# How many weight slices the first pass of layer one takes in the first three blocks of tokens: 3, 4 and 6 in place of 5, 5 and 7

## The chip, the cores and the metric

The kernel runs on one core of a Trainium2 chip. The metric is the time of one execution on the device in microseconds (us). The core's engines are called as the profile calls them: PE (matrix products; PEld are its weight loads), DVE (vector), ACT (activations), POOL (GpSimd) and SP, whose queue issues every DMA of this kernel.

## The reference

Attention over 8 batches of 576 tokens, 8 heads of 64, whose keys and values are first averaged in groups of 8 (so 72 keys per head), and two feed-forward layers behind it, all in fp32:

```python
scores = scale * q @ mean8(k).T ; attn = softmax(scores) ; x = attn @ mean8(v)
x = x.transpose(0, 2, 1, 3).reshape(4608, 512)      # tokens x (heads * 64)
h = x @ w_in1 ; x = (h * cos(h)) @ w_out1           # 512 -> 2048 -> 512
h = x @ w_in2 ; out = (h * clip(h + 3, 0, 6) / 6) @ w_out2
```

The weights arrive as 64-bit floating-point numbers, read as pairs of 32-bit words.

## The kernel before, in words

The 4608 tokens are cut into 9 blocks of 512, which don't coincide with the batches of 576. A block of a layer needs all 16 slices of 128 of the 2048 hidden features. One slice of one block is a *step*: a first GEMM (`gemm1`, line 175) of 12 matmuls, the activation, and two steps later a second GEMM (`gemm2`, line 237) of 12 matmuls, which adds into the block's four accumulators. It is 12 since every operand is split into a high and a low part (4 chunks, 3 products each). A step is also two half-steps, called slots: the even one has the first GEMM of step s, the odd one the second GEMM of step s - 2.

The activation of a step of layer one is three operations of ACT (lines 185, 195, 199), two of DVE (196, 209), the high part on ACT (212) and the low part (218) on POOL, or on DVE for the step numbers listed in `GLD`. ACT uses Sin there and Exp in the attention, and loads a table whenever it changes between them.

Layer one goes over the blocks twice. Pass one (the list `NAL`) takes the first slices of each block, `NAL[block]` of them, and stores the partial sums to memory. Pass two takes the rest, adds the partial sums and stores the layer's result. The reason is room: while the attention is live, there is space for the converted weights of 7 slices only. Layer two then takes all 16 slices of each block.

A weight slice has two halves. A half is fetched (512 KB, `fetch_weights`, two in flight) and converted (`convert_weights`) from the 64-bit words to a high and a low part: four operations of DVE (lines 116, 120, 125, 128), two of ACT (115, 133) and one of POOL (134). When that happens follows three things: a count of attention pieces for the first six halves (`WPRE`), due slots for the next five (`WAT`, line 53: 5, 10, 13, 13, 19), and need: a step whose slice isn't whole yet converts it at once, and each step also asks for the next step's slice (`need`, lines 613 to 619, called on lines 667 and 674). After the attention the rest is converted one operation to a slot (`w_ahead`).

The attention is a generator of 253 pieces (a piece ends at each `yield` of lines 514 to 547): scores, exponentials, normalisation, transposes, and the product with v, whose result is stored to memory as x (line 503) and fetched again by blocks (line 145), split in a high and a low part by ACT (152) and POOL (153). The keys and values pass through one buffer each in turn (line 334 averages them on DVE). 39 pieces come before step 0. From then on each slot lets the generator run up to a goal, which depends on the block and on how far the block has come:

```python
goal = base + 32 * (key[1] + (2 * i + odd + 1 + PACE) / (2 * NAL[key[1]]))   # line 708
goal += GOFF[slot]                                                           # line 712
```

`key[1]` is the block, `i` the step within it, `base` is 39. So 32 pieces go to each block, whatever its number of steps. The x of the next block is fetched when at most four steps of the block are left and the batch that it needs is done (lines 688 to 691).

The order of writing is a wish. A planner puts the instructions on each engine in an order of its own ahead of time, by that order and by what it expects to be ready, so that matmuls of a later step stand between those of the attention.

Of the kernel before, what the change touches and what calls it, by code (L numbers as in the profile page):

```python
# [29 lines left out]
def tile_kernel(ctx, tc, q, k, v, wi1, wo1, wi2, wo2, ident_d, mask_d, out):  # L30
# [8 lines left out]
    NF = wo1.shape[0] // P  # L39
    NB = NT // N  # L40
    NA = 7
    NAL = [5, 5, 7, 7, 7, 7, 7, 7, 7]
    LAG = 2
    GLD = [18, 23, 24, 28, 30, 37, 38, 39, 40, 41, 42, 43, 44, 45, 46, 47, 48, 49, 50, 51, 52, 53, 54, 55, 56, 57, 58, 60, 61, 62, 63, *range(64, 999)]
    LEAD = 1
# [514 lines left out]
    for bl in range(NB):  # L560
        n = NAL[bl]
        steps += [(0, (0, bl), bl, fc, fc == 0, fc == n - 1) for fc in range(n)]
    SA = len(steps)
    for bl in range(NB):
        n = NAL[bl]
        steps += [(0, (1, bl), bl, fc, fc == n, fc == NF - 1) for fc in range(n, NF)]
# [94 lines left out]
    for slot in range(2 * (T + LAG) + 4):  # L661
# [43 lines left out]
        if live:  # L705
            key = steps[s][1]
            i = sum(1 for x in steps[:s] if x[1] == key)
            goal = base + 32 * (key[1] + (2 * i + odd + 1 + PACE) / (2 * NAL[key[1]]))
            if key[0] > 0:
# [65 lines left out]
```

## Time and profile before

| | before |
|---|---|
| median of 3 runs | 1803.48 us (1799.16 to 1804.42) |
| profiled execution | 1801.62 us |
| its span, first to last instruction | 1799.8 us |
| DVE, ACT, POOL busy | 896.4, 891.6, 393.8 us |

The page cuts the span into 40 slices of 45 us; a digit is the busy share of a slice in tenths:

```profile
PE   5689999999999999999999999999999999999999
DVE  6998656656777656654446852222222222222222
ACT  3588878787666655555556543232323222232222
POOL 2755444222223222221112421010101000010000
```

The attention is live in the first ten slices, layer one's second pass and layer two take the rest. Matmuls overlap in the profile, so a PE digit of 9 may hide a matmul that is short of its pace; a busy share is compared with that of other stretches, not with one.

### The profile page before, as it was taken

The page shows a single profiled execution, that of the slowest core. Times are in us where ns is not written, and L with a number is a line of the kernel's source. Part 1 is how long each engine was busy: PE and PEld are TensorE (multiplying, and loading weights), DVE is VectorE, ACT ScalarE, POOL GpSimd, SP SyncE. Part 2 cuts the span into 40 slices and gives each one's busy share as a digit, 9 for nine tenths or more (in the row PEclk, how much of TensorE's full clock was granted, in tenths as well). Part 3 has the DMA queues.
Part 4 walks back from the last instruction along what each step waited for, and adds up shares of the span by engine and source line. Part 5 has one row for each costly group of instructions (what it writes and reads, how often), then busy time and mean ns, then how long its engine had stood idle before and what let it go on. Part 6 is the DMA issues. An engine that isn't in the chain of part 4 may idle for free.

```text
span 1799.8 us, 21002 instructions
## 1 busy us (share of the span) xinstructions
PE 1739.2 (97%) x7952; PEld 1429.5 (79%) x7952; DVE 896.4 (50%) x1398; ACT 891.6 (50%) x1508; POOL 393.8 (22%) x320
## 2 busy tenths in 40 slices
PE   5689999999999999999999999999999999999999
PEld 4567777788888888888888788888888888888887
DVE  6998656656777656654446852222222222222222
ACT  3588878787666655555556543232323222232222
POOL 2755444222223222221112421010101000010000
PEclk7799999999999999999999999999999999999999
DMA  7656442323333313222223411010101010100000
GB/s 196 194 172 195 143 136 74 118 83 103 117 105 118 106 59 105 97 85 76 71 70 106 140 59 47 1 47 1 47 1 48 0 47 8 40 18 24 0 24 24
DMA packets 115077, 139.84 MB, mean 78 GB/s; under 512 B 44192, under 2 KB 68896, under 8 KB 114976
## 3 DMA queue, kind: packets, MB, share of 16 engines
q1 hardware_dynamic: 114976, 138.51, 24.8%
q8 instruction: 62, 1.02, 0.2%
q14 instruction: 39, 0.32, 0.1%
HBM read 100.73 MB, written 37.75 MB: 77 GB/s over the span
## 4 chain that ended last, share of the span: by engine, by line
PE 85%; DVE 6%; DMA 3%; POOL 2%; ACT 2%; issue 2%; SPq 0%; DVEq 0%; POOLq 0%; ACTq 0%
PE y L237 40%; PE h L175 40%; PE ap_ps L494 1%; PE ap_ps L407 1%; DVE raw L334 1%; DMA raw<-in_k_dram 1%; DMA raw<-in_v_dram 1%; POOL xl L153 1%; DVE sm L429 1%; DVE g L196 1%; POOL e L433 1%; DVE a L125 1%; PE ap_ps L393 0%; PE ap_ps L459 0%; DVE sm L430 0%
## 5 line engine op out<-in xcount | busy, mean ns | idle before, releaser
L175 PE MATMUL h<-xl,wh 128*128 128x512 f32 x1152 | 451.3, 392 | 4.2 <-POOL xl L153 4.2
L175 PE MATMUL h<-xh,wh 128*128 128x512 f32 x1152 | 453.5, 394 | 0.5 <-DVE g L209 0.5
L175 PE MATMUL h<-xh,wl 128*128 128x512 f32 x1152 | 450.8, 391 | 0.0
L201 DVE SCALAR_TENSOR_TENSOR g<-g,h 128x512 f32<-128x512 f32 x144 | 99.3, 689 | 454.7 <-ACT g L187 454.7
L153 POOL TENSOR_TENSOR xl<-xr,xh 128x512 fp32r<-128x512 f32 x108 | 153.3, 1438 | 779.2 <-ACT xh L152 778.1
L187 ACT ACTIVATE g<-h,bias_c 128x512 f32<-128x512 f32 x144 | 99.0, 687 | 409.7 <-PE h L175 409.3
L218 DVE TENSOR_TENSOR gl<-g,gh 128x512 fp32r<-128x512 f32 x255 | 190.3, 746 | 157.7 <-ACT gh L212 154.4
L212 ACT ACTIVATE gh<-g 128x512 fp32r<-128x512 f32 x288 | 181.6, 630 | 175.2 <-DVE g L201 104.5
L175 PEld LDWEIGHTS h<-xl,wh 128*128 128x128 f32 x1152 | 216.7, 188 | 50.2 <-POOL xl L153 6.5
L175 PEld LDWEIGHTS h<-xh,wh 128*128 128x128 f32 x1152 | 216.9, 188 | 45.5 <-issue 1.2
L175 PEld LDWEIGHTS h<-xh,wl 128*128 128x128 f32 x1152 | 216.9, 188 | 44.3
L237 PE MATMUL y<-gh,wh 128*128 128x512 f32 x576 | 226.7, 394 | 0.0
L237 PE MATMUL y<-gl,wh 128*128 128x512 f32 x576 | 226.6, 393 | 0.0
L237 PE MATMUL y<-gh,wl 128*128 128x512 f32 x576 | 225.6, 392 | 0.0
L237 PE MATMUL y<-wh,gh 128*128 128x512 f32 x576 | 224.3, 389 | 1.1 <-DVE yv L245 1.1
L237 PE MATMUL y<-wh,gl 128*128 128x512 f32 x576 | 224.1, 389 | 0.0
L237 PE MATMUL y<-wl,gh 128*128 128x512 f32 x576 | 224.1, 389 | 0.0
L196 DVE SCALAR_TENSOR_TENSOR g<-g,t 128x512 f32<-128x512 f32 x144 | 112.6, 783 | 149.8 <-ACT g L195 149.5
L134 POOL TENSOR_TENSOR wl<-a,wh 128x512 fp32r<-128x512 f32 x64 | 88.4, 1381 | 269.4 <-ACT wh L133 269.4
L237 PEld LDWEIGHTS y<-wh,gh 128*128 128x128 f32 x576 | 108.2, 188 | 24.4 <-DVE yv L245 1.9
L199 ACT ACTIVATE g<-g 128x512 f32<-128x512 f32 x144 | 91.0, 632 | 72.9 <-DVE g L196 72.5
L237 PEld LDWEIGHTS y<-wh,gl 128*128 128x128 f32 x576 | 108.1, 188 | 22.5
(110 smaller groups left out, 2086.1 us busy)
## 6 DMA issues: line engine op xcount, KB each, us to landing
xr<-x_d SPq DMA_DIRECT2D x72, 256.0 KB, 3.2
st<-in_moe_w_in_dram SPq DMA_DIRECT2D x32, 512.0 KB, 6.6
st<-in_moe_w_out_dram SPq DMA_DIRECT2D x32, 512.0 KB, 4.1
yp_d<-ys SPq DMA_DIRECT2D x36, 256.0 KB, 2.4
yv<-yp_d SPq DMA_DIRECT2D x36, 256.0 KB, 3.4
xr<-y_d SPq DMA_DIRECT2D x36, 256.0 KB, 2.7
out_dram<-ys SPq DMA_DIRECT2D x36, 256.0 KB, 2.0
raw<-in_k_dram SPq DMA_DIRECT2D x8, 1024.0 KB, 5.7
```

The costliest lines, as they stand in the source:

```text
L125: nc.vector.scalar_tensor_tensor(out=a, in0=hi, scalar=0xC0000000, in1=a, op0=ALU.bitwise_and, op1=ALU.bitwise_or)
L134: nc.gpsimd.tensor_tensor(out=wl, in0=w, in1=f(wh), op=ALU.subtract)
L153: nc.gpsimd.tensor_tensor(out=xl, in0=t, in1=f(xh), op=ALU.subtract)
L175: nc.tensor.matmul(h, a[:, cs], z, start=(n == 0), stop=(n == 3 * NC - 1))
L187: nc.scalar.activation(out=g, in_=hs[s], func=AF.Relu, bias=bias_c[:, 2:3], scale=1.0)
L196: mark[s] = nc.vector.scalar_tensor_tensor(out=g, in0=g, scalar=MAGIC, in1=t, op0=ALU.subtract, op1=ALU.subtract)
L199: nc.scalar.activation(out=g, in_=g, func=AF.Sin, scale=-TWO_PI)
L201: mark[s] = nc.vector.scalar_tensor_tensor(out=g, in0=g, scalar=6.0, in1=h, op0=ALU.min, op1=ALU.mult)
L212: nc.scalar.activation(out=gh, in_=g, func=AF.Copy)
L218: eng.tensor_tensor(out=gl, in0=gs[s][0], in1=f(gh), op=ALU.subtract)
L237: nc.tensor.matmul(y[c], a, z, start=(first and n == 0), stop=(last and n == 2))
L334: eng.tensor_tensor(out=t[:, :, :w], in0=t[:, :, :w], in1=t[:, :, w : 2 * w], op=ALU.add)
```

## The change

`NAL` gives the slices per block of pass one. Pass two takes the slices that pass one has left, so blocks 0, 1 and 2 have 13, 12 and 10 there in place of 11, 11 and 9. Step numbers and slots behind block 0 move to other work, and with them the lists that go by them (`GLD`, `WAT`, `GOFF`), which are not changed.

```diff
     NB = NT // N
     NA = 7
-    NAL = [5, 5, 7, 7, 7, 7, 7, 7, 7]
+    NAL = [3, 4, 6, 7, 7, 7, 7, 7, 7]
     LAG = 2
```

## Rows read from the trace of the kernel before

**Rows 1.** The page: busy time of each engine, and the chain that ended last.
```profile
PE 1739.2 (97%) x7952; PEld 1429.5 (79%) x7952; DVE 896.4 (50%) x1398; ACT 891.6 (50%) x1508; POOL 393.8 (22%) x320
PE 85%; DVE 6%; DMA 3%; POOL 2%; ACT 2%; issue 2%; SPq 0%; DVEq 0%; POOLq 0%; ACTq 0%
```

**Rows 2.** Windows: stretch and its us, busy us of each engine, PEclk, DMA share, GB/s.
```profile
75.40:132.10 56.70, 47.99 (x230) 37.80 (x229) 53.30 (x83) 40.94 (x75) 33.23 (x28) 0.88 0.59 176
132.10:182.10 50.00, 46.12 (x251) 35.88 (x249) 44.52 (x74) 41.88 (x77) 27.91 (x25) 1.00 0.63 195
182.10:245.40 63.30, 58.91 (x310) 46.70 (x309) 40.07 (x73) 51.35 (x91) 35.14 (x32) 1.00 0.43 128
245.40:445.00 199.60, 194.33 (x1027) 158.53 (x1027) 121.53 (x229) 160.22 (x275) 59.52 (x57) 1.00 0.32 99
445.00:1799.80 1354.80, 1350.00 (x5953) 1116.85 (x5951) 577.72 (x832) 564.84 (x926) 204.70 (x147) 1.00 0.18 57
```

**Rows 3.** Timeline of PE: first matmuls of steps 0, 5 and 10.
```profile
75.44 0.79 PE L175 MATMUL h<-xh,wh 128*128 128x512 f32 x1
...
132.13 0.39 PE L175 MATMUL h<-xh,wh 128*128 128x512 f32 x1
...
182.05 0.50 PE L175 MATMUL h<-xh,wh 128*128 128x512 f32 x1
```

**Rows 4.** Chain in order of time, 100 to 260 us: start, us, what.
```profile
116.46 4.23 DMA x_d<-xs
...
175.99 5.36 DMA xr<-x_d
...
182.07 1.21 POOL xl L153
...
245.44 1.59 PE h L175 x6
```

**Rows 5.** Windows: the three stretches of blocks 0 to 2 as one.
```profile
75.40:245.40 170.00, 153.01 (x788) 120.38 (x786) 137.89 (x228) 134.17 (x241) 96.29 (x83) 0.96 0.54 164
```

**Rows 6.** Chain in order of time, around 745 us: one first and one second GEMM.
```profile
744.50 2.72 PE h L175 x12
747.22 2.72 PE y L237 x12
```

**Rows 7.** Groups of DVE, 75.4 to 245.4 us: busy us, mean ns, idle before.
```profile
L196 DVE SCALAR_TENSOR_TENSOR g<-g,t 128x512 f32<-128x512 f32 x17 | 17.4, 1026 | 9.3 <-ACT g L195 9.3
L209 DVE TENSOR_TENSOR g<-h,g 128x512 f32<-128x512 f32 x16 | 11.0, 685 | 5.5 <-ACT g L199 5.4
L125 DVE SCALAR_TENSOR_TENSOR a<-st,a 128x512 uint32<-128x512 uint32 x9 | 9.9, 1099 | 0.1
L120 DVE SCALAR_TENSOR_TENSOR a<-st,a 128x512 uint32<-128x512 uint32 x9 | 8.2, 916 | 0.1
L128 DVE SCALAR_TENSOR_TENSOR a<-e,a 128x512 f32<-128x512 bf16 x9 | 6.8, 756 | 0.0
L116 DVE TENSOR_SCALAR a<-st 128x512 uint32<-128x512 uint32 x8 | 6.0, 744 | 2.3 <-POOL wl L134 2.3
```

**Rows 8.** Groups of ACT, 75.4 to 245.4 us.
```profile
L199 ACT ACT_TABLE_LOAD x12 | 15.4, 1283 | 0.2
L423 ACT ACT_TABLE_LOAD x11 | 14.1, 1283 | 1.3 <-DVE e L418 1.1
L185 ACT ACTIVATE t<-h 128x512 f32<-128x512 f32 x17 | 10.2, 598 | 6.8 <-PE h L175 6.7
L212 ACT ACTIVATE gh<-g 128x512 fp32r<-128x512 f32 x16 | 10.0, 626 | 6.3 <-DVE g L209 6.2
```

**Rows 9.** Groups of POOL, 75.4 to 245.4 us.
```profile
L218 POOL TENSOR_TENSOR gl<-g,gh 128x512 fp32r<-128x512 f32 x16 | 23.0, 1438 | 33.0 <-ACT gh L212 33.0
L134 POOL TENSOR_TENSOR wl<-a,wh 128x512 fp32r<-128x512 f32 x9 | 13.0, 1447 | 4.4 <-ACT wh L133 4.4
```

**Rows 10.** Windows: the 655 us behind the attention.
```profile
445.00:1100.00 655.00, 653.92 (x2883) 540.63 (x2882) 389.94 (x560) 371.08 (x628) 171.58 (x121) 1.00 0.29 94
```

**Rows 11.** Group of DVE line 196, 445 to 1100 us.
```profile
L196 DVE SCALAR_TENSOR_TENSOR g<-g,t 128x512 f32<-128x512 f32 x103 | 75.4, 732 | 128.2 <-ACT g L195 128.2
```

## The prediction

> **What bounds the kernel now.** I read the page first, then the windows cut at the starts of the blocks, then the groups of the first stretch, then the chain in order of time. The page has PE busy for 97% of the span and on 85% of the chain that ended last [rows 1]: PE is the bound, and what a change is worth is what it does to PE's lost time. The windows show where that is [rows 2]. From 445.0 us on PE is busy 1350.00 of 1354.80 us. From 245.4 to 445.0 it is busy 194.33 of 199.60. The loss lies ahead of that. Counting line 175's matmuls in twelves gives the starts of the first-GEMM steps: step 0 at 75.4, step 5 (block 1) at 132.1, step 10 (block 2) at 182.1, step 17 (block 3) at 245.4 [rows 3, 4]. Before 75.4 there is only attention, and it is written in the same order after the change. In the 170.0 us of blocks 0 to 2 PE is busy 153.01, DVE 137.89, ACT 134.17, POOL 96.29 us [rows 5]: PE loses 17.0 us, and DVE comes close behind. In block 0's stretch alone DVE is busy 53.30 of 56.70 us (94%), PE 47.99 (85%); in block 1's, DVE 44.52 of 50.00 (89%), PE 46.12 (92%) [rows 2]. So for the first 100 us after step 0 DVE is as much the bound as PE, while after 445 it is busy 577.72 of 1354.80 us (43%). Work moved from there to the end leaves the scarce engine for one with room, but costs PE its full price at the end.
>
> **What the change does, part by part.** Blocks 0, 1 and 2 have 3+4+6 = 13 steps in place of 17 in pass one; pass two of the same blocks has 13+12+10 = 35 in place of 31. The total stays at 288 steps, and loads of x, loads and stores of partial sums, conversions and attention keep their counts. The goal formula sets the attention by the block and not by the step: by its counters block 1 starts after 93 pieces of attention in place of 87, block 2 after 119 in place of 116, block 3 after 144 in place of 145. Between two steps of block 0 there is more attention; the ends of the blocks meet the same attention as before. Attention ends with the third step of block 6 before and after, so what follows is the same list with four steps more.
>
> *PE, moved to the end.* In the full stretch a first GEMM of 12 matmuls takes 2.72 us and a second one 2.72 [rows 6]: a step is 5.44 us, four are +21.8 us, on the path. Their vector work there is hidden: ACT, DVE and POOL have 57%, 58% and 85% idle after 445.0 [rows 2]. If that cover were gone, the steps would cost the same matmuls plus waits, which those rows don't show.
>
> *PE, gone from the first stretch.* 153.01 - 21.8 = 131.2 us are left.
>
> *DVE, gone from the first stretch.* Each step has line 196 (1026 ns there) and line 209 (685 ns): four are 6.8 us. Conversions follow need: two halves of a weight slice (slice 6) move to block 3. A half is four DVE operations, 744 + 916 + 1099 + 756 ns = 3.5 us; two are 7.0 us [rows 7]. Together 13.8, which leaves 124.1 us. Moreover slices 3 and 4 are converted later within the stretch: before, the third and fourth steps force all four halves early in block 0 (14 us of DVE, in the 94% stretch); after, the due times 5, 10, 13 and 13 spread them over blocks 0 and 1.
>
> *ACT and POOL.* ACT loses four operations of about 0.62 us per step, 9.9 us, and per step about 1.35 of the 1.28 us table loads (23 loads to 17 steps), 6.9 us [rows 8]. POOL loses four line 218 of 1438 ns and two line 134 of 1447 ns, 8.6 us [rows 9], leaving 87.7. Neither was the bound.
>
> *Queues.* A moved step issues no DMA. A converted half lets the next 512 KB fetch go: those of slices 4 to 6 stand later in SP's queue, behind more of the attention's loads and x stores, and are needed later by as much. In pass two the slices from 7 on are converted one operation to a half-step from the end of attention: by the counters slice 15 is ready 7 half-steps ahead of its use in place of 4. No wait is added there. The lists by step number (GLD) and by half-step (GOFF) meet other attention than before; that is an edit whose price no row shows. I bound it by the idle of blocks 3 to 6, 199.60 - 194.33 = 5.3 us [rows 2], either way, and take nothing, since per block that idle is under 1.5 us.
>
> **The sum.** What counts is how long the shortened stretch lasts: its 131.2 us of PE work over the share that PE reaches. The best case is 97.4%, as in the stretch from 245.4 to 445.0 [rows 2]: 134.7 us, which DVE's 124.1 us would fill to 92%, below the 94% seen. That is 35.3 shorter, less 21.8: -13.5 us. The worst is block 0's share, 84.6% [rows 2]: 155.1 us, 14.9 shorter, +6.9 us. The share follows how DVE and PE stand to each other: block 0's stretch has 1.11 us of DVE to one of PE and reaches 84.6%; block 1's has 0.965 and reaches 92.2%. After the change it is 124.1 / 131.2 = 0.946, nearest to block 1's. I take 92.2%: 131.2 / 0.922 = 142.3 us, 27.7 shorter, less 21.8: **-5.9 us**. The profiled execution took 1801.62 us (span 1799.8) and would take 1795.7. The median of the runs is 1803.48, 1.9 above it: 1797.6 us.
>
> Against this stands one thing in the rows: POOL's share of the shorter stretch rises from 96.29 / 170.0 = 57% to 87.7 / 142.3 = 62%, and DVE's line 196 takes 1026 ns there against 732 from 445 to 1100 us, where POOL is busy 171.58 of 655.00 us (26%) [rows 5, 7, 10, 11]. The Trainium skill, "SBUF — State Buffer", section "Who interferes with whom", says that a DVE instruction with two SBUF inputs and a GpSimd instruction that reads SBUF share a read interface, and the second to issue blocks. The trace agrees in direction. By that rule 294 ns for 30 points of POOL would be 0.05 us for 5 more points, on the 34 such operations that remain at lines 196, 120, 125 and 128: 1.6 us of DVE, and the sum would be about -4.3 instead of -5.9.
>
> **The rivals.**
>
> *Nothing measurable.* PE paces the stretch and its 17.0 us of loss belong to the attention, a fixed number of bubbles per batch. For it: blocks 1 and 2 already run PE at 92% and 93%, with DVE at 63% in block 2's [rows 2]. Against: DVE's 94% in block 0's. Then the loss stays between 17.0 us and the 14.6 that PE's mean share of 90.0% would leave: 0 to -2.4 us, 1801.1 to 1803.5.
>
> *Slower: block 0 runs out of matmuls.* Block 1 cannot start before the second batch's attention has gone out to memory and come back. Before, the last store on the chain begins at 116.46 us, and step 5 starts only at 132.13, some 11 us after it has landed [rows 3, 4]; block 2's x likewise: fetch at 175.99, split on POOL at 182.07, step 10 at 182.05 [rows 3, 4]. Before, steps 3 and 4 fill the wait; after, block 0 has 6 half-steps in all, against 9 that ran in its stretch: 3 x 2.72 = 8.2 us of matmuls are missing. If batch 1 ends sooner by less than that, the rest is idle PE. The conversions that leave block 0's path (three halves by its end, 10.5 us) decide: against the rival if they all lie on the path to batch 1, for it if PE or DMA paces that path. If none does, the price is 8.2 us, plus a granted clock that stays low longer: it was 0.88 in that stretch and 1.00 in the later ones [rows 2], and a fall to 0.80 on some 40 us of PE work would be 4 us. With half of both: +6, 1809.5.
>
> **How the numbers follow.** Under 0.3%, 5.4 us, can't be told from no change. Forecast (DVE gives way): 0.45, own range 1790 (the best case of the sum) to 1798. Nothing measurable: 0.34. Slower: 0.21, 1809 to 1815. The range 1787 to 1811 takes the best case with 3 us of the unpriced lists, and the worst of the sum (1803.5 + 6.9 = 1810.4). Faster 0.45, same 0.34, slower 0.21.
>
> **What would show it.** Right: step 13 (block 3) starts near 218 us in place of 245, PE above 91% from step 0 to there, DVE below 90%, conversions of slices 3 and 4 spread past block 0, and everything behind the attention alike but 21.8 us longer. Wrong: block 1's start stays past 127 us with PE idle ahead of it (rival two), or PE's loss in the stretch is again 15 to 17 us (rival one), or waits for x at the starts of the blocks exceed those of before.

## The result: slower by 0.6%

The changed kernel takes 1811.87 us (median of 4 runs, 1810.2 to 1813.66) against 1801.69 (4 runs) before: a ratio of 1.0061, 95% interval 1.0049 to 1.0073. The forecast was 1797.6. The span of its profiled execution is 1811.1 us, 11.3 more than before. The page answers to [rows 1] with these lines:

```profile
PE 1744.1 (96%) x7952; PEld 1432.7 (79%) x7952; DVE 894.4 (49%) x1398; ACT 889.2 (49%) x1504; POOL 393.7 (22%) x320
PE 82%; DVE 6%; ACT 4%; DMA 3%; issue 2%; POOL 2%; SPq 0%; DVEq 0%; POOLq 0%; ACTq 0%
```

PE's share of the chain fell from 85 to 82%: more of the time goes by without PE setting the end. The windows, cut at the starts of blocks 0 (75.4; its first matmul is at 76.1), 1, 2 and 3 and at the fourth step of block 6, where the attention has ended, show where, beside [rows 2]. Columns: stretch and its us, busy us of PE, PEld, DVE, ACT, POOL, PEclk, DMA share, GB/s.

```profile
75.40:129.30 53.90, 41.63 (x200) 31.71 (x199) 50.71 (x77) 36.12 (x70) 32.25 (x26) 0.88 0.66 194
129.30:181.10 51.80, 45.98 (x230) 37.09 (x231) 44.70 (x76) 37.51 (x69) 27.91 (x25) 0.88 0.63 184
...
181.10:232.80 51.70, 47.41 (x258) 37.03 (x256) 35.13 (x65) 42.60 (x78) 29.61 (x27) 1.00 0.49 148
232.80:433.90 201.10, 196.52 (x1036) 159.08 (x1036) 123.75 (x234) 165.04 (x283) 67.02 (x61) 1.00 0.32 98
433.90:1811.10 1377.20, 1372.20 (x6048) 1135.09 (x6048) 581.53 (x842) 575.58 (x942) 203.71 (x148) 1.00 0.18 56
```

Behind the attention the kernel is 1377.2 - 1354.8 = 22.4 us longer: the four steps at their full price. From block 3 to that step it takes 201.1 us in place of 199.6. So blocks 0 to 2 had to give back more than 22 us, and give 170.0 - 156.7 = 13.3. Of that, 11.6 come from block 2 (63.3 to 51.7). Blocks 0 and 1 have seven steps in place of ten, 16 us less of matmuls, and block 2 starts at 181.1 us in place of 182.1. Block 1 starts at 129.3 in place of 132.1. The timeline of PE ahead of that start (start, us, what, idle before and who ended it):

```profile
121.56 0.71 PE L407 MATMUL ap_ps<-kbd,qT 128*128 128x144 f32 x4
124.11 0.73 PE L407 MATMUL ap_ps<-kbd,qT 128*128 128x144 f32 x4 [1.84 <-DVE e L418]
124.68 0.60 PE L393 MATMUL ap_ps<-ident,qm 128*128 128x128 f32 x4
125.97 0.66 PE L459 MATMUL ap_ps<-ident,e 128*128 128x128 f32 x4 [0.69 <-ACT qT L395]
127.42 0.76 PE L407 MATMUL ap_ps<-kbd,qT 128*128 128x144 f32 x4 [0.80 <-DVE e L418]
129.29 1.22 PE L175 MATMUL h<-xh,wh 128*128 128x512 f32 x2 [1.11 <-ACT xh L152]
```

Block 0's six half-steps are done, and PE has only small matmuls of the attention. The scores of line 407 wait for line 418 though they don't read what it writes: line 418 is the last reader of the PSUM bank that they are to fill. That is the commonest wait of PE from 75.4 to 181 us in this kernel (us in total, times, longest):

```profile
PE ap_ps L407 <- DVE e L418: 4.0, 3, 1.8
PE ap_ps L494 <- ACT xs L502: 3.9, 2, 2.2
PE h L175 <- POOL xl L153: 2.0, 2, 1.7
PE ap_ps L459 <- ACT kbd L345: 2.0, 2, 1.2
PE ap_ps L459 <- ACT qT L395: 1.1, 2, 0.7
```

Four of these five are waits for one of the two banks that all pieces of the attention share (`ap_ps`), 11.0 us together, and the third is the wait for x. A count of the copies of line 502, eight to a batch, tells how fast the attention goes. First after, then before (stretch and its us, ACT busy in that line and the count):

```profile
72.00:125.50 53.50, 3.27 (x8) 0.87 0.66 196
125.50:176.50 51.00, 3.24 (x8) 0.87 0.61 178
```

```profile
72.00:125.50 53.50, 3.12 (x8) 0.90 0.60 177
125.50:176.50 51.00, 3.13 (x8) 0.97 0.60 185
```

Batches 1 and 2 end where they ended before, some 52 us apart, whether ten steps of the layer lie beside them or seven: from the last copy of batch 0 to the last of batch 2 it is 104.9 us in both kernels, here before and after.

```profile
70.70:175.60 104.90, 6.25 (x16) 0.93 0.60 181
```

```profile
70.90:175.80 104.90, 6.52 (x16) 0.87 0.64 189
```

### The profile page after: what moved, and what is told of

Its sections match the earlier page's. It is cut to its first block, busy times and chain, and to the rows that moved or that the text cites. A ratio compares the mean times of both kernels' runs of the same rounds, so it can differ in the third digit from the quotient of the medians.

```text
span 1811.1 us, 20989 instructions
## 1 busy us (share of the span) xinstructions
PE 1744.1 (96%) x7952; PEld 1432.7 (79%) x7952; DVE 894.4 (49%) x1398; ACT 889.2 (49%) x1504; POOL 393.7 (22%) x320
## 4 chain that ended last, share of the span: by engine, by line
PE 82%; DVE 6%; ACT 4%; DMA 3%; issue 2%; POOL 2%; SPq 0%; DVEq 0%; POOLq 0%; ACTq 0%
PE y L237 39%; PE h L175 39%; PE ap_ps L407 2%; PE ap_ps L494 2%; DMA raw<-in_v_dram 1%; DVE raw L334 1%; DVE a L125 1%; DMA raw<-in_k_dram 1%; DVE a L128 1%; ACT g L195 1%; ACT t L185 1%; PE ap_ps L459 1%; DMA xr<-x_d 1%; PE ap_ps L393 1%; ACT gh L212 0%
## 5 line engine op out<-in xcount | busy, mean ns | idle before, releaser
L237 PEld LDWEIGHTS y<-gl,wh 128*128 128x128 f32 x576 | 108.8, 189 | 22.8 <-POOL gl L218 1.3
```

The source lines that it names most:

```text
L237: nc.tensor.matmul(y[c], a, z, start=(first and n == 0), stop=(last and n == 2))
```

## The experiments

Theory A, formed from these rows: batches 1 and 2 have a pace of their own, which PE's other work doesn't set, so a step that leaves blocks 0 and 1 buys next to nothing there and costs 5.4 us at the end. Its rivals: block 0 alone starves while block 1's x is on its way (B), and the lists by step and slot no longer fit (C). Which resource sets the pace was open; in later expectations, P is theory A with the attention's two banks as what sets it, and A' is A with any other cause. All ratios are to the kernel before, run beside each variant (its medians lie between 1799.64 and 1800.65 us), with 95% intervals.

| run | median us | ratio |
|---|---|---|
| e1_block0 (3, 5, 7) | 1812.4 | 1.0065 [1.0052, 1.0077] |
| e2_block1 (5, 4, 7) | 1802.88 | 1.0012 [1.0003, 1.0020] |
| e3_block2 (5, 5, 6) | 1798.66 | 0.9988 [0.9979, 0.9997] |
| e4_more (6, 6, 7) | 1805.82 | 1.0032 [1.0021, 1.0044] |
| e15_555 (5, 5, 5) | 1800.54 | 1.0006 [0.9996, 1.0015] |
| e5_conv_held | 1819.86 | 1.0104 [1.0091, 1.0118] |
| e6_conv_half | 1811.91 | 1.0062 [1.0050, 1.0074] |
| e7_before_conv_half | 1801.9 | 1.0012 [1.0003, 1.0021] |
| e8_x1_free | 1813.89 | 1.0071 [1.0059, 1.0083] |
| e13_lists_moved | 1812.81 | 1.0071 [1.0058, 1.0083] |
| e11_after_2acc | 1815.79 | 1.0089 [1.0076, 1.0103] |
| e9_after_2acc_4banks | 1804.38 | 1.0025 [1.0016, 1.0033] |
| e12_before_2acc | 1807.4 | 1.0051 [1.0037, 1.0065] |
| e10_before_2acc_4banks | 1791.78 | 0.9965 [0.9952, 0.9978] |
| e14_lists_moved_4banks | 1807.55 | 1.0047 [1.0035, 1.0060] |
| e16_4banks_conv_half | 1798.14 | 0.9989 [0.9980, 0.9998] |
| e17_before_4banks_conv_half | 1799.76 | 1.0001 [0.9993, 1.0010] |
| e18_4banks_x1_free | 1803.98 | 1.0024 [1.0015, 1.0033] |

### Which block costs it

```diff
-    NAL = [5, 5, 7, 7, 7, 7, 7, 7, 7]
+    NAL = [3, 5, 7, 7, 7, 7, 7, 7, 7]   # e1; e2: 5, 4, 7; e3: 5, 5, 6; e4: 6, 6, 7; e15: 5, 5, 5
```

e1: 

> Blocks 0 to 2 take 3, 5 and 7 slices: the change in block 0 alone, two steps (10.9 us) moved behind the attention. Theory A (the attention of batches 1 and 2 has a pace of its own, some 52 us a batch, whatever steps lie beside it): block 1 still starts near 129 us and block 2 near 182, so nearly all of the 10.9 comes through: +7 to +11 us. Theory B (only block 0 is short of matmuls while it waits for block 1's x): +8 to +11 as well, but then the other two parts cost nothing. Theory C (each step costs the same, some 2.6 us, because the lists by slot no longer fit): +5.

e2: 

> Blocks 0 to 2 take 5, 4 and 7 slices: one step (5.4 us) moved out of block 1. Theory A: batch 2 ends at 175 us as before, block 2 starts at 181 or 182: +3 to +5.4 us. Theory B: 0. Theory C: +2.6.

e3: 

> Blocks 0 to 2 take 5, 5 and 6 slices: one step moved out of block 2, where PE is busy 93% and DVE 63%. Theory A: PE paces this block, so the block gets shorter by at least the step: -3 to 0 us. Theory B: 0. Theory C: +2.6.

e4: 

> The other way: blocks 0 to 2 take 6, 6 and 7 slices, two steps (10.9 us) moved forward into blocks 0 and 1. Theory A with a pace that is the attention's own chain (latencies): block 1 and block 2 start as before, 132 and 182 us, and the steps fill PE's idle time: -4 to -10 us. Theory A with DVE as the pace-maker: two steps' vector work (3.4 us) and slice 5's conversion (7 us) come into the stretch where DVE is busy 94%, and the blocks get longer by about as much as is moved: -2 to +3 us.

e15: 

> Blocks 0 to 2 take 5, 5 and 5 slices: block 2, where taking one step gave -2.0 us, gives two. Theory P (PE paces block 2 as long as its work is longer than the attention's 44 to 52 us): the first step bought more than its 5.4 us, the second brings block 2 to some 50 us, at the attention's pace: -3 to +2 us against the kernel before. Theory C: +5.

Block 0's two steps carry the whole loss (+11.8 us between the medians); block 1's one costs 2.2, block 2's gives 2.0: together 12.0, near the change's 10.2 between its medians. Theory C's even price of 2.6 us a step is out. e1's blocks 0 and 1:

```profile
75.60:128.80 53.20, 41.12 (x198) 31.30 (x196) 49.58 (x75) 36.06 (x69) 31.49 (x26) 0.88 0.66 194
128.80:180.00 51.20, 45.36 (x225) 36.55 (x226) 43.34 (x76) 37.31 (x69) 28.07 (x25) 0.87 0.59 175
```

Two steps less buy 3.5 us in block 0 and cost 1.2 in block 1, which has the same five steps as before. The other way, e4's first two blocks, with six steps each:

```profile
75.80:137.60 61.80, 50.37 (x245) 38.94 (x245) 57.77 (x85) 44.15 (x79) 37.61 (x31) 0.93 0.59 177
137.60:195.90 58.30, 53.46 (x290) 42.26 (x288) 45.57 (x80) 48.87 (x87) 32.39 (x28) 1.00 0.55 166
```

They are 5.1 and 8.3 us longer, and the total is 5.2 us longer, outside both ranges on record: two steps more don't fill idle time there. With 12, 10, 9, 8 and 7 steps in blocks 0 and 1, block 2 starts at 195.9 (e4), 182.1, 175.6 (e2), 180.0 (e1) and 181.1 us: down to nine steps the stretch follows the work, below that it doesn't. e2 missed theory A's forecast, in which block 2 starts at 181 or 182 us: block 1's step bought 6.5 us there, for 5.4 at the end. Number and place of the steps change together in these runs (the nine are 5 and 4, the eight 3 and 5), so that the limit lies at the number is not shown; with 5 steps in block 0 a step of block 1 buys time, with 3 it buys none. Block 2 follows its steps all the way from seven (63.3 us before) to six and five, in e3 and e15:

```profile
181.50:237.20 55.70, 52.57 (x276) 41.20 (x275) 37.20 (x65) 45.63 (x81) 29.10 (x27) 1.00 0.44 133
```

```profile
181.60:231.50 49.90, 47.47 (x254) 36.80 (x254) 36.30 (x64) 42.23 (x77) 29.29 (x26) 1.00 0.50 148
```

5, 5, 6 is the one version with the full computation that beats both kernels, by 0.12% of the kernel before; its interval ends at 0.9997. The second step out of block 2 lost that again.

### Is DVE the pace-maker?

e5 holds the conversions of slices 3 to 6 back on DVE; e6 and e7 leave two of the four DVE operations out for slices 2 to 6, in the changed kernel and in the one before.

```diff
+        at = max(mark, default=0) - 1                      # e5, in w_convert
+        if n and m == 0 and 3 <= fc < NA and at in mark:
+            with tc.issue_after(mark[at].ins):
+                w_ops(n)
...
-        w = f(a)
+        w, leave = f(a), m == 0 and 2 <= fc < NA            # e6, e7
-            nc.vector.scalar_tensor_tensor(                 # lines 120 and 125
+            leave or nc.vector.scalar_tensor_tensor(
```

e5: 

> The changed kernel (3, 4, 6), with the conversions of slices 3 to 6 held on DVE behind line 196 of the step before the one beside which they are written. Block 0 loses three halves of conversion (some 10 us of DVE) that the planner pulls ahead there. Theory A with DVE as pace-maker: batch 1 ends 5 to 10 us before 123.9 and block 1 starts as much before 129.3; total 3 to 8 us under the changed kernel, i.e. +3 to +8 against the kernel before. Theory A with the attention's own chain as pace: batch 1 ends at 122 to 125 again, total +10 to +14. Theory B (wait for x, whatever paces it): as A, the total follows block 1's start.

e6: 

> The changed kernel, where two of the four DVE operations (lines 120 and 125) of each conversion of layer one's slices 2 to 6 are left out: ten halves, some 2 us each. Theory A with DVE as pace-maker: batch 1 ends 6 to 9 us earlier, batch 2 some 14 to 16 us earlier than with them, total -8 to -14 us against the changed kernel (0 +-4 against the kernel before). Theory A with its own chain as pace: batch ends within 3 us of 123.9 and 175.7, total within 3 us of the changed kernel.

e7: 

> The kernel before, with the same two operations left out of slices 2 to 6. Theory A with DVE as pace-maker of block 0: batch 1 ends 5 to 9 us earlier here too, but PE has more work there (85% busy), so the total falls by less than in the changed kernel: -3 to -8 us. Chain: within 3 us of the kernel before.

DVE alone doesn't set the length of the three blocks. Block 0 in e5 and in e6:

```profile
75.80:134.00 58.20, 44.48 (x196) 33.87 (x195) 38.85 (x65) 33.03 (x63) 26.15 (x25) 0.80 0.56 159
```

```profile
74.60:129.20 54.60, 40.21 (x200) 30.13 (x199) 41.96 (x72) 40.78 (x75) 29.51 (x27) 0.91 0.69 204
```

In e6 DVE is busy 77% of block 0, PE 74%, ACT 75%, and block 1 starts at 129.2 us as with the full conversions at 129.3. In e5 DVE falls to 67%, and block 1 starts later. The three blocks as one, in e5 and e6:

```profile
75.80:233.40 157.60, 134.60 (x677) 104.52 (x677) 117.88 (x202) 111.83 (x209) 82.87 (x74) 0.92 0.56 168
74.60:231.50 156.90, 130.08 (x684) 101.39 (x683) 110.74 (x200) 119.01 (x217) 82.94 (x77) 0.96 0.61 178
```

DVE's work is 117.9 and 110.7 us there in place of the changed kernel's 130.6, and the blocks last as long as its 156.7. e5 missed both of its ranges: it is 8 us slower than the changed kernel, and the loss lies behind block 2 (from block 3 to the fourth step of block 6 it takes 209.4 us in place of 201.1), where held conversions then stand. The batches move singly: in e6 the second ends at 172.5 us in place of 175.7 and block 2 starts 4.2 us sooner, but lasts 54.6 us in place of 51.7. In e7 the first batch ends at 114.5 us in place of 121.2, as the forecast for a DVE that paces block 0 had it, and block 1 starts 7.4 us sooner (step 0 alone 3.1 of it); block 2 starts at 182.6 us as before, and the total stays within 2 us. What DVE's 94% in block 0 held was in good part conversions and averages that the planner had put into its free time. The Trainium skill, "Perfetto Trace Analysis", section "Identifying the Most-Contended Engine", says to improve first the engine with the highest occupancy, with busy share as the measure for VectorE. Here the runs differ from it: a sixth less of DVE's work in that stretch bought nothing in the total.

### Is it the wait for x, or the lists by step and slot?

```diff
-        ... in_=src[c * P : (c + 1) * P, bl * N : (bl + 1) * N])                  # e8: block 1 reads block 0's x
+        ... in_=src[c * P : (c + 1) * P, (bl, 0)[key == (0, 1)] * N : ...])
-                ready = nk[0] != 0 or min(...) in done
+                ready = nk[0] != 0 or nk == (0, 1) or min(...) in done
...
-    GLD = [18, 23, 24, 28, 30, 37, ...]                                            # e13
+    GLD = [14, 19, 20, 24, 26, 33, 34, 35, 36, 37, ...]
-    GOFF = ...
+    GOFF = GOFF[0:6] + GOFF[10:18] + GOFF[20:32] + GOFF[34:]     # written out
```

e8: 

> The changed kernel, where block 1 reads block 0's x, so that its steps need not wait for batch 1 to go out and come back. Theory B (block 0 has too few matmuls while x of block 1 is on its way): block 1's first step starts before 115 us in place of 129.3, PE's idle time from 103 to 129 us goes, total 6 to 11 us under the changed kernel. Theory A (the attention's pace decides, steps ahead of time only take DVE and ACT from it): block 1 starts early, but block 2 no more than 3 us earlier than 181.1, and the total falls by under 3 us.

e13: 

> The changed kernel, with GLD and GOFF moved along with the steps (entries of the steps and half-steps that left blocks 0 to 2 are taken out), so that from block 3 on each step meets the entries that it had before. Theory C (part of the loss is that the lists no longer fit): 3 to 10 us under the changed kernel. Theory P (the attention's two PSUM banks pace batches 1 and 2, and what leaves blocks 0 and 1 buys no time there): within 3 us of the changed kernel, batches 1 and 2 end at 124 and 176 us again.

Neither. In e8 block 1 starts 22 us sooner, at 107.4, and block 2 at 180.1, 1.0 us sooner:

```profile
75.10:107.40 32.30, 25.81 (x116) 19.66 (x116) 28.81 (x40) 22.24 (x44) 25.35 (x19) 0.83 0.67 200
107.40:180.10 72.70, 60.14 (x317) 47.69 (x315) 67.77 (x114) 54.05 (x100) 36.72 (x33) 0.95 0.62 189
```

What PE does early it then doesn't have later: the wait moves from the end of block 0 to the end of block 1, where batch 2 is due. e13's 1812.81 us is the changed kernel's time. No run changed the goal of 32 pieces to a block, by which the attention is written beside the steps; that it takes part in the pace is not excluded.

### Is it the two PSUM banks?

The pieces of the attention share two banks (`piece`, once the first block may start). To give them four, the second GEMM is cut to two accumulators (its output then isn't the reference's); e11 and e12 are the controls, with two accumulators and two banks. The scores ahead of step 0 come from the same banks, and step 0 starts 2.0 us (e9) and 3.5 us (e10) sooner than in the controls.

```diff
-            yps[key] = [ps_y.tile([P, N], F32, tag=f"y{c}", name=f"y{c}") for c in range(NC)]
+            yps[key] = [ps_y.tile([P, N], F32, tag=f"y{c}", name=f"y{c}") for c in range(2)] * 2
...
-            return ps_a.tile([P, N], F32, tag="ap", name="ap_ps", bufs=2)
+            return ps_a.tile([P, N], F32, tag="ap", name="ap_ps", bufs=4)      # e9, e10
```

e11: 

> Control: the changed kernel with two accumulators for the second GEMM in place of four (chunks 0 and 2 add into one bank, 1 and 3 into the other; the output is not the reference's), so that two PSUM banks are left over and not used. The copies out of the accumulators stand behind all of a step's matmuls, at 27 ends of blocks. All theories: the changed kernel's time plus 0 to 25 us; batch 1 ends within 3 us of 123.9.

e12: 

> Control: the kernel before with the same two accumulators. All theories: 8 to 14 us under e11_after_2acc.

e9: 

> As e11_after_2acc, and the two PSUM banks that it leaves over go to the attention, whose pieces then share four banks in place of two. Theory P (the attention's pace is set by its two banks: a piece can only start on PE when the piece two before it has been copied out by ACT or DVE): batches 1 and 2 take under 46 us in place of 52, block 1 starts before 122 us, the total falls by 8 to 20 us against e11_after_2acc. Theory A' (any other latency of the attention's chain, or the planner's order): batches 1 and 2 within 3 us of 52, total within 4 us of e11_after_2acc.

e10: 

> As e12_before_2acc, with four banks for the attention. Theory P: the total falls, but by less than in the changed kernel, where PE lost more to it: -4 to -12 us against e12_before_2acc, and the difference between 3, 4, 6 and 5, 5, 7 shrinks from 11 to under 5 us. Theory A': within 4 us of e12_before_2acc, difference 8 to 14.

With 3, 4, 6 the pace moves with the banks. In e9 batch 1 is out at 104.9 us, with the same engines and the same work that took until 124.5 in e11. Batches 1 and 2 together, from the end of batch 0, by the copies of x (line 503 in these kernels), in e11 and e9 (3, 4, 6; two banks and four) and in e12 and e10 (5, 5, 7); columns: stretch and its us, ACT busy in that line and the count, PEclk, DMA share, GB/s:

```profile
72.90:175.40 102.50, 6.53 (x16) 0.90 0.63 191
71.10:147.70 76.60, 6.31 (x16) 0.98 0.66 195
```

```profile
73.80:177.00 103.20, 6.27 (x16) 0.97 0.61 184
70.30:168.80 98.50, 5.79 (x16) 0.97 0.57 177
```

With two banks they take as long beside seven steps as beside ten; with four, 21.9 us less beside seven. The two banks don't make 52 us a batch by themselves, though: batch 3 took 44.4 us in the changed kernel with the same banks, beside block 2. What acts together with them is not shown. Both versions gain, 1815.79 to 1804.38 and 1807.4 to 1791.78 us, 5, 5, 7 by more than its range. Blocks 0 to 2 of e9, and then of e10, each with its stretch to block 6:

```profile
74.80:120.30 45.50, 39.02 (x231) 31.23 (x232) 41.39 (x78) 37.87 (x74) 28.74 (x27) 1.00 0.66 195
120.30:163.00 42.70, 34.93 (x185) 27.77 (x183) 33.20 (x61) 31.91 (x55) 23.73 (x21) 0.96 0.65 183
163.00:219.00 56.00, 49.91 (x257) 41.41 (x257) 48.51 (x75) 45.43 (x85) 33.41 (x29) 0.97 0.64 196
219.00:417.10 198.10, 191.98 (x1032) 160.48 (x1031) 126.42 (x236) 166.59 (x286) 69.09 (x63) 1.00 0.32 101
```

```profile
74.00:127.30 53.30, 42.79 (x223) 33.23 (x223) 50.57 (x78) 38.49 (x73) 31.97 (x27) 0.97 0.55 169
127.30:181.00 53.70, 49.00 (x263) 39.40 (x263) 46.63 (x83) 44.49 (x77) 31.65 (x28) 0.97 0.61 195
181.00:238.20 57.20, 55.33 (x293) 45.60 (x291) 40.53 (x70) 49.56 (x88) 31.55 (x30) 1.00 0.49 151
238.20:429.30 191.10, 190.18 (x1022) 160.09 (x1022) 118.92 (x229) 160.34 (x277) 62.14 (x57) 1.00 0.33 104
```

And blocks 0 to 2 as one in e11 and in e12:

```profile
76.80:231.70 154.90, 133.49 (x682) 104.03 (x680) 129.36 (x214) 116.95 (x215) 91.42 (x77) 0.93 0.59 180
```

```profile
77.50:245.40 167.90, 150.46 (x785) 117.89 (x785) 139.34 (x228) 134.86 (x241) 97.49 (x83) 0.98 0.55 167
```

With four banks the three blocks are 164.2 - 144.2 = 20.0 us shorter with 3, 4, 6 than with 5, 5, 7; with two they are 13.0 shorter in the controls, and 13.3 in the two kernels. So two banks are a large part of what kept the steps from buying time there. The Trainium skill, "Perfetto Trace Analysis", section "Optimization Strategy", says that a gap that keeps repeating on the engine that should be full can mean too few buffers in SBUF or PSUM; these runs agree, by the 7.0 us.

But the expectation that the difference in the total would shrink failed: between the medians it is 12.6 us, and 8.4 in the controls. What four banks gave behind block 2 is 2.8 us with 3, 4, 6 and 8.7 with 5, 5, 7. In the profiled executions the difference is 9.6 us: 21.8 at the end, 7.0 from block 3 to the fourth step of block 6 and 0.8 ahead of step 0, less the 20.0; e9's is the fastest of its eleven runs. The last four runs asked why.

e14, e9 with e13's lists: 

> e9_after_2acc_4banks (3, 4, 6, two accumulators, four banks for the attention) with the same moved lists. There blocks 0 to 2 gave back 20.0 of the 21.8 us, but blocks 3 to 6 took 198.1 us against 191.1. Theory C: that second loss goes, 5 to 9 us under e9, +0 to +4 against e10. Without C (the attention of batches 4 to 7 has no spare pace beside PE either): within 3 us of e9.

e16, e9 with e6's conversions: 

> e9_after_2acc_4banks (3, 4, 6, four banks) with two DVE operations left out of each conversion of slices 2 to 6, as in e6. If DVE is what paces once the banks don't (with four banks six of these halves are converted after 163 us, in blocks 2 and 3): 6 to 14 us under e9. If not: within 3 us of e9.

e17, e10 with them: 

> e10_before_2acc_4banks with the same operations left out. If DVE paces then: 2 to 8 us under e10, less than in the 3, 4, 6 version, so that the difference between the two falls from 12.6 to under 8 us. If not: within 3 us of e10, difference 10 to 15.

e18, e9 with e8's x: 

> e9_after_2acc_4banks where block 1 reads block 0's x, as in e8. With four banks batch 1 ends at 104.9 us and block 1 starts only at 120.3. If that wait for x is what the 3, 4, 6 version still loses: block 1 starts before 108 us and the total falls by 5 to 10 us against e9. If the attention's pace decides: within 3 us of e9.

The lists are not it (3 us slower), nor is x (0.4 us faster). With the cheap conversions 3, 4, 6 gains 6.2 us, the total that a DVE as the next pace-maker would give, and 3, 4, 6 is then 1.6 us the faster. But batches 1 and 2 don't bear that out: they take 83.2 us there in place of 76.6. And the difference is gone also since 5, 5, 7 loses 8.0 us with less work to do, which no theory here has. That an order which the planner makes anew for each variant is worth that much is a guess that no run tests. In e9 PE's wait for the split of x on POOL is its longest from 75 to 245 us (8.3 us, 4.2 in e11), and e18 frees block 1's x alone. Why four banks don't close the gap stays open.

## Why the prediction was wrong

**What held.** The four steps at the end: 21.8 us forecast, 22.4 measured. Blocks 3 to 6 alike: 201.1 against 199.6 us. The list of what would show it wrong named what came: "block 1's start stays past 127 us with PE idle ahead of it".

**The step that failed** is the sum's rule that the shortened stretch lasts "its 131.2 us of PE work over the share that PE reaches", with the share taken from block 1's 92.2%. What ran:

```profile
75.40:232.80 157.40, 135.01 (x684) 105.83 (x683) 130.55 (x216) 116.23 (x215) 89.77 (x77) 0.92 0.59 176
```

PE is busy 135.0 of the 157.4 us, 85.8%. The stretch got 13.3 us shorter and not 27.7. Those 14.4 us that didn't come, 0.6 more at the end, 1.5 in blocks 3 to 6 and 0.7 ahead of step 0 add up to the 17.2 us between the forecast's -5.9 and the +11.3 of the spans. Two terms were off: the share, and the 131.2 us of PE work, which are 135.0 at a mean granted clock of 0.92 in place of 0.96 [rows 5]; at 92.2% the 3.8 us more would make some 4 of the 14.4, the share makes the rest. In e6 PE's work is 130.1 us, as forecast, at a clock of 0.96, and the stretch lasts as long: idle time took its place. A busy share of 92% came about because ten steps happened to fill the time that the attention of two batches takes anyway, 104.9 us with either list. It was an outcome of the mix and not a rate at which a smaller mix is worked off. That the two banks are part of what sets this time is shown (76.6 us with four, beside seven steps); the rest is open. The forecast's other end, block 0's 84.6% and +6.9 us, came nearer because it carried that idle time along.

**DVE's relief**, which was to shorten the stretch, failed twice. The conversions did not leave it: line 128, one to a half, from 75.4 to 232.8 us, beside the nine of [rows 7]:

```profile
L128 DVE SCALAR_TENSOR_TENSOR a<-e,a 128x512 f32<-128x512 bf16 x9 | 6.4, 711 | 0.0
```

Nine halves and nine: slice 6's two did not move to block 3, and of the three halves that were to leave block 0 one did. The planner had put slice 6's ahead, at 168.6 and 182.3 us, though they are written beside block 3. DVE's work in the three blocks fell from 137.9 to 130.6 us, 7.3 and not 13.8. And where it fell further, to 117.9 and 110.7 us in e5 and e6, the stretch was no shorter. That DVE is busy 94% of a stretch was read as a bound; the total did not hang on what filled it.

**The rivals.** The second, "block 0 runs out of matmuls", had the place and nearly the size (1809.5 forecast for it, 1811.87 measured), at a chance of 0.21. Against its own baseline, a loss that stays at 17.0 us, it added 4.1 us for missing matmuls and 2 for the clock; measured are 22.4 - 17.0 = 5.4 us more idle PE and 3.8 us more PE work, and with 0.6 and 1.5 further on these make the +11.3. So its terms were right in kind. Its reason, the wait for block 1's x, is not enough: with x at hand (e8) the time stays, and the wait comes one block later. What lies behind it is the attention's pace; PE without matmuls is how that shows. Its clock part was seen: the clock fell in the first half of block 1, behind the gap,

```profile
118.90:129.30 10.40, 5.96 (x40) 4.98 (x38) 9.27 (x13) 8.12 (x18) 6.47 (x6) 0.96 0.83 270
129.30:155.40 26.10, 22.72 (x104) 18.24 (x105) 20.65 (x39) 15.25 (x32) 13.65 (x13) 0.75 0.59 178
```

but in e6 it was granted in full from 129.2 to 176.9 us, block 1 was 4.1 us shorter, and the total was the same. The first rival, a loss of PE that stays at 17.0 us, was wrong by what the loss did: idle time in the three blocks rose to 157.4 - 135.0 = 22.4 us with less to do. The rule on the SBUF port, cited there from the Trainium skill, "SBUF — State Buffer", section "Who interferes with whom", moved the sum by 1.6 us and could not have decided anything; POOL's share was 89.77 of 157.40 us, 57% as before and not 62%, so this run doesn't test it.

## What to carry to other kernels

Before work is moved out of a stretch, find what sets the stretch's length without that work: count the progress of the other stream (here eight copies to a batch) against the time, in two versions that put different work beside it. An engine that is busy 94% is a bound only if someone waits for it; waits on a buffer's last reader, spread over four lines of a few us each, pointed to the two banks here, and four banks made the three blocks 10.7 us shorter with 3, 4, 6. Steps are best taken from the block whose length follows its steps (block 2: 63.3, 55.7, 49.9 us), and left in those that last as long without them; here even that bought 2 us and no more, since each step costs 5.4 us at the end. And one edit gives the planner a new order everywhere: the same operations left out in two versions gave -6.2 and +8.0 us, so a difference of a few us between two variants of such a kernel doesn't name its cause.

## What the runs showed of the hardware

DVE's load in block 0 could be cut from 94% to 77% (e6) or 67% (e5) with no gain in the total. PE ran the 26.1 us behind a stretch of 10.4 us, in which it was busy 5.96, at a mean granted clock of 0.75, that is partly at the lower of its two levels; in e6 it ran block 1 at 1.00, in 47.7 us in place of 51.8, and block 2's 54.6 in place of 51.7 took most of that back.
